# Pooled attention with a gated feed-forward: the order of all instructions read from a table instead of computed by a list scheduler

## The chip, the core and the metric

One core of a Trainium2 chip runs the whole kernel. The metric is device time in microseconds (us). The kernel was timed in three runs; one more execution was profiled, and all rows below come from that one.

## What is computed

Queries are averaged over pairs of neighbouring positions, attention is computed for 4 batches of 8 heads (1152 keys, 576 pooled queries, 64 wide), and the result goes through a feed-forward network with a convolution of three taps and a sigmoid gate:

```python
q_pool = q.reshape(B, H, S // 2, 2, D).mean(axis=3)
scores = (1 / np.sqrt(D)) * np.matmul(q_pool, k.transpose(0, 1, 3, 2))
attn = softmax(scores)                      # max, exp, divide by the sum
x = np.matmul(attn, v) -> (B, 576, 512)     # heads side by side
h = np.maximum(x @ w_in, 0.0)               # 512 -> 1024
conv_out[s] = sum_k conv_w[k] * h[s + k - 1]
out = (h * sigmoid(conv_out)) @ w_out       # 1024 -> 512
```

## The kernel before

The work is cut into 2149 tasks. A task belongs to one engine and issues one instruction or a short run of them (a DMA task belongs to SP, whose queue issues all DMAs). Sixteen pairs of heads are handled one after the other, four to a batch; pairs overlap in time.

For each pair SP loads keys (`load_k`), queries (`load_q`) and values (`load_v`). `sum_q` adds the two neighbouring queries, `keep_q` scales them, `swap` copies them by DMA to the other half of the partitions (tile `qd`). Nine blocks of scores follow. For each block PE writes 128 x 1152 scores into PSUM tile `s` (line 474), DVE takes the row maximum (`top`, line 486), ACT the exponential (`expo`, line 491), and then the slot of `s` is free again. `s` has two slots, so the third block's matmuls wait for the first block's exponential. DVE turns sums into reciprocals (`inverse`, lines 504 and 508).

The probabilities must then be transposed. For most heads ACT or POOL writes a float16 high part (`high`: line 533 on ACT, line 528 on POOL), DVE the low part (`low`, line 536), and SP transposes both by DMA (line 549). For the seven heads in `X32` the block is normalised in float32 (`norm`, line 568, POOL or DVE), PE transposes it (line 581) and ACT copies it out of PSUM tile `a` (line 586). `values` multiplies with V (lines 611 and 617). Values are split into high and low parts too (`abs_v`, `spread_v`, `top_v`, `hi_v`, `lo_v`).

When four pairs are done, `feed` multiplies with `w_in` (line 652) and does relu, `tap0` (ACT or POOL), two more taps (line 675), tanh and the gate; `second` multiplies with `w_out` (line 718 and 724), copies out (`keep`, line 732) and stores. Before that, 17 pieces of weights are converted from 64-bit to 32-bit floats by `weights`: a load, then ACT `size`, DVE `clamp` and three `bits` (lines 784, 793, 798, 802), ACT `rest`, DVE `join` (line 815), POOL `join` (line 817).

Every engine executes its tasks strictly in one fixed order. `Plan.order` makes that order when the program is built: every task has a key (a constant of `AT` plus the number of its pair), a duration written by hand, and its dependences; a list scheduler picks, again and again, the ready task of the lowest key on the engine that can begin first, and gives each buffer the slot that comes free first. Which of the tasks that could run on two engines go where is set by the lists `HIGH` and `MORE`. A buffer taken again waits for all users of the slot's last holder.

Of the kernel before, what the change touches and what calls it, by code (L numbers as in the profile page):

```python
# [16 lines left out]

# [12 lines left out]
class Ring:  # L30


    def __init__(self, name, n, pool, shape, dtype, lead=False):
        self.name, self.n, self.pool, self.shape, self.dtype = name, n, pool, shape, dtype
        self.slots = [None] * n
        self.queue = []
        self.lead = lead


class Buf:  # L40


    def __init__(self, ring, order=None):
        self.ring, self.users, self.slot, self.t = ring, [], None, None
        self.order = order
# [12 lines left out]
class Task:  # L58
    def __init__(self, key, engine, ns, fn, after=(), uses=(), takes=(), port=False, dma=0.0, mode=0):
        self.key, self.engine, self.ns, self.fn = key, engine, ns, fn  # L60
        self.after, self.uses, self.takes = list(after), list(uses), list(takes)
        self.port, self.dma, self.mode = port, dma, mode
        self.start = self.end = None
        for b in self.uses + self.takes:
            b.users.append(self)


class Plan:


    HOP = 0.09
    LOOK = 0.25
    SWITCH = 0.1
    DRAIN = 0.05
# [9 lines left out]
    def order(self):  # L84
        free = {}
        mode = 0
        dma = 0.0
        held = {"POOL": 0.0, "DVE": 0.0}
        other = {"POOL": "DVE", "DVE": "POOL"}
        left = sorted(self.tasks, key=lambda t: t.key)  # L90
        for t in left:
            for b in t.takes:
                for u in b.users:
                    if u is not t and t not in u.after:
                        u.after.append(t)
        for n, t in enumerate(left):
            t.rank = n
            t.wait = len(t.after)
            t.ready = 0.0
            t.next = []  # L100
        for t in left:
            for a in t.after:
                a.next.append(t)
        for t in left:
            for b in t.takes:
                b.ring.queue.append(b)
        ready = [t for t in left if not t.wait]
        done = []

        def slot_time(t):  # L110
            worst, picks, used = 0.0, [], {}
            for b in t.takes:
                r = b.ring
                k = used.get(r, 0)
                if r.lead and r.queue[k] is not b:
                    return None
                used[r] = k + 1
                best = None
                for i, old in enumerate(r.slots):
                    if (r, i) in picks:  # L120
                        continue
                    if old is None:
                        at = 0.0
                    elif any(u.end is None for u in old.users):
                        continue
                    else:
                        at = max(u.end for u in old.users) + self.HOP
                    if best is None or at < best[0]:
                        best = (at, i)
                if best is None:  # L130
                    return None
                picks.append((r, best[1]))
                worst = max(worst, best[0])
            return worst, picks

        while ready:
            could = []
            for t in ready:
                s = slot_time(t)
                if s is None:  # L140
                    continue
                at = max(t.ready, s[0], free.get(t.engine, 0.0))
                if t.port:
                    at = max(at, held[other[t.engine]])
                could.append((at, t, s[1]))
            if not could:
                raise RuntimeError("no task can begin: " + ", ".join(str(t.key) for t in ready[:9]))
            first = {}
            for at, t, p in could:
                e = first.get(t.engine)  # L150
                if e is None or at < e:
                    first[t.engine] = at
            pick = min(
                (c for c in could if c[0] <= first[c[1].engine] + self.LOOK),
                key=lambda c: (
                    first[c[1].engine],
                    c[1].key - (AT["stay"] if c[1].engine == "PE" and c[1].mode == mode else 0.0),
                    c[1].rank,
                ),
            )  # L160
            at, t, picks = pick
            t.start = at
            busy = at + t.ns
            if t.engine == "PE":
                busy += self.SWITCH * (t.mode != mode)
                mode = t.mode
            if t.port:
                held[t.engine] = busy
            free[t.engine] = busy
            t.end = busy  # L170
            if t.dma:
                dma = max(dma, at + 1.4) + t.dma
                t.end = dma + 1.1
            for b, (r, i) in zip(t.takes, picks):
                b.slot = i
                r.slots[i] = b
                r.queue.remove(b)
            ready.remove(t)
            done.append(t)
            for n in t.next:  # L180
                n.wait -= 1
                hop = self.HOP if n.engine != t.engine or t.dma else 0.0 if n.engine == "PE" else 0.08
                if t.engine == "PE" and n.engine != "PE":
                    hop += self.DRAIN
                n.ready = max(n.ready, t.end + hop)
                if not n.wait:
                    ready.append(n)
        if len(done) != len(left):
            raise RuntimeError("tasks left")
        done.sort(key=lambda t: t.start)  # L190
        return done

AT = {
    "first_v": -552.65, "load": -571.72, "load_v": -328.63, "turn_k": -136.13, "turn_q": -82.52,
    "abs_v": -120.27, "hi_v": -89.34, "lo_v": -340.13, "sum_q": 171.08, "turn_p": -295.04, "mm": -898.8,
    "top": 127.29, "exp": -1.46, "inv": 15.15, "high": -11.73, "low": -9.95, "pv": -231.88, "f1": 62.48,
    "f1_step": 0.05, "f2": 240.2, "f2_step": 157.77, "g1": 86.75, "g1_step": 0, "g2": 97.99, "g2_step": 0.4,
    "end": 82.52, "wi": 3.33, "wi_step": 3.68, "wo": 29.25, "wo_step": 10.18, "stay": 246.22,
}

HIGH = [1, 0, 3, 3, 1, 4, 0, 3, 9, 3, 0, 0, 0, 0, 3, 1]

MORE = {
    "norm": [8, 5, 3, 9, 9, 8, 8, 3, 8, 8, 8, 5, 2, 7, 9, 0],
    "tap0": [6, 2, 4, 1, 0, 7, 1, 7],
    "hi_v": [1, 0, 0, 1, 0, 1, 1, 0, 0, 0, 0, 1, 1, 1, 1, 0],
    "sum_q": [1, 1, 1, 1, 0, 0, 0, 0, 1, 1, 1, 1, 1, 0, 0, 1],  # L210
}
X32 = {(0, 0), (1, 0), (2, 0), (3, 1), (4, 1), (5, 1), (8, 0)}
# [3 lines left out]
def tile_pooled_attention_conv_gate_ffn(  # L216
# [10 lines left out]
    nc = tc.nc  # L227
# [30 lines left out]
    r_s = Ring("s", 2, ps, [P, 3 * 512], F32, lead=True)  # L258
    r_a = Ring("a", 2, ps, [P, 512], F32)
    r_vin = Ring("vin", 1, sb, [P, 2, NC, D], F32, lead=True)  # L260
    r_qin = Ring("qin", 1, sb, [P, 2, K0], F32, lead=True)
    r_kt = Ring("kt", 3, sb, [P, S], F32, lead=True)
    r_qt = Ring("qt", 2, sb, [P, K0], F32, lead=True)
    r_qd = Ring("qd", 2, sb, [P, K1], F32, lead=True)
    r_v = Ring("v", 2, sb, [P, 2, NC, P], F16, lead=True)
    r_p = Ring("p", 3, sb, [P, S], F32, lead=True)
    r_hl = Ring("hl", 4, sb, [P, 2, S], F16, lead=True)
    r_pt = Ring("pt", 4, sb, [P, 2 * NC, 320], F16, lead=True)
    r_sm = Ring("sm", 4, sb, [P, 8], F32, lead=True)
    r_vs = Ring("vs", 3, sb, [P, 8], F32, lead=True)  # L270
    r_x = Ring("x", 7, sb, [P, 578], F32, lead=True)
    r_h = Ring("h", 5, sb, [P, 324], F32)
    r_g = Ring("g", 4, sb, [P, 4, 322], F32, lead=True)
# [20 lines left out]
    for pr in range(NPAIR):  # L294
        o = Pair()
        o.b, o.h0, o.k0 = pr // NP, 2 * (pr % NP), 9 * pr
        o.pr, o.vin, o.qin = pr, Buf(r_vin), Buf(r_qin)
        o.kt, o.qt, o.qd = Buf(r_kt), Buf(r_qt), Buf(r_qd)

        o.x32 = [(pr, e) in X32 for e in range(2)]  # L300
        o.v, o.vs = Buf(r_v), Buf(r_vs)
        o.x = Buf(r_x)
        pairs.append(o)

    def loads(o):
        k0 = o.k0
# [14 lines left out]
        lk = [add(k0 + AT["load"], "SP", 0.3, load_k, takes=[o.kt], dma=2.1)]  # L321
# [431 lines left out]
    def weights(src, j, c, key, ready):  # L753
# [67 lines left out]
        if key > AT["wi"]:  # L821
            gated.append(t)
# [101 lines left out]
```

## Time and profile before

| what | us |
|---|---|
| median of three runs | 677.12 (674.49 to 678.02) |
| the profiled execution, its own time | 677.61 |
| its span, first to last instruction | 675.6 |
| mean granted TensorE clock, share of 2.4 GHz | 0.975 |

Two microseconds lie outside the span. An engine's busy time is the time in which at least one of its instructions runs; instructions overlap a little, so sums of durations are some per cent above it. A wait is put down to the instruction that came last.

### The profile page before, as it was taken

The page shows a single profiled execution, that of the slowest core. Times are in us where ns is not written, and L with a number is a line of the kernel's source. Part 1 is how long each engine was busy: PE and PEld are TensorE (multiplying, and loading weights), DVE is VectorE, ACT ScalarE, POOL GpSimd, SP SyncE. Part 2 cuts the span into 40 slices and gives each one's busy share as a digit, 9 for nine tenths or more (in the row PEclk, how much of TensorE's full clock was granted, in tenths as well). Part 3 has the DMA queues.
Part 4 walks back from the last instruction along what each step waited for, and adds up shares of the span by engine and source line. Part 5 has one row for each costly group of instructions (what it writes and reads, how often), then busy time and mean ns, then how long its engine had stood idle before and what let it go on. Part 6 is the DMA issues. An engine that isn't in the chain of part 4 may idle for free.

```text
span 675.6 us, 10454 instructions
## 1 busy us (share of the span) xinstructions
PE 628.2 (93%) x3805; PEld 385.2 (57%) x3805; DVE 538.0 (80%) x797; ACT 477.7 (71%) x789; POOL 161.9 (24%) x183
## 2 busy tenths in 40 slices
PE   4778788899989999999999899999999999999997
PEld 2455555465656656456666566556666655568643
DVE  3888887889899899977889899888788999745610
ACT  3898856688878888676777787876868777745401
POOL 2543423234452412115433010010100412000200
PEclk9899976699999999999999999999999999999999
DMA  7897956569696699799989989899898999991001
GB/s 271 214 199 137 249 142 169 122 158 211 130 216 166 134 209 204 124 209 201 188 159 228 185 171 211 145 229 200 176 211 164 188 178 168 179 178 38 0 16 54
DMA packets 279123, 113.72 MB, mean 168 GB/s; under 512 B 265377, under 2 KB 265889, under 8 KB 279073
## 3 DMA queue, kind: packets, MB, share of 16 engines
q1 hardware_dynamic: 279072, 113.07, 80.1%
q8 instruction: 30, 0.49, 0.3%
q14 instruction: 21, 0.16, 0.1%
HBM read 37.77 MB, written 4.72 MB: 63 GB/s over the span
## 4 chain that ended last, share of the span: by engine, by line
PE 67%; DVE 12%; ACT 11%; issue 5%; DMA 3%; POOL 1%; SPq 0%; ACTq 0%; DVEq 0%; POOLq 0%
PE s L474 19%; PE a L718 16%; PE a L652 13%; PE a L611 10%; ACT p L491 5%; PE a L617 5%; DVE sm L486 4%; DVE hl L536 4%; PE a L581 3%; ACT pt L586 2%; PE a L724 2%; ACT hl L533 2%; DVE g L675 1%; DMA pt<-hl 1%; DMA qd<-qt 1%
## 5 line engine op out<-in xcount | busy, mean ns | idle before, releaser
L474 PE MATMUL s<-kt,qt 64*128 64x512 f32 (+3 forms) x704 | 192.1, 486 | 31.9 <-ACT p L491 24.0
L486 DVE TENSOR_REDUCE sm<-s 128x1 f32<-128x1152 f32 x144 | 193.1, 1350 | 28.8 <-PE s L474 28.0
L491 ACT ACTIVATE p<-s,sm 128x1152 f32<-128x1152 f32 x144 | 175.1, 1217 | 57.6 <-DVE sm L486 34.6
L536 DVE SCALAR_TENSOR_TENSOR hl<-p,sm,hl 128x1152 f16<-128x1152 f32 (+1 forms) x116 | 167.6, 1457 | 14.2 <-ACT hl L533 9.7
L474 PEld LDWEIGHTS s<-kt,qt 64*128 64x128 f32 (+1 forms) x704 | 92.0, 178 | 148.0 <-issue 87.1
L474 PE MATMUL s<-kt,qd 64*128 64x512 f32 x256 | 147.4, 662 | 0.2 <-DMA qd<-qt 0.2
L652 PE MATMUL a<-x,wi 128*128 128x257 f32 (+1 forms) x512 | 135.0, 414 | 1.8 <-ACT x L624 1.1
L533 ACT ACTIVATE hl<-p,sm 128x1152 f16<-128x1152 f32 (+1 forms) x96 | 118.5, 1247 | 9.3 <-issue 3.2
L611 PE MATMUL a<-pt,v 128*64 128x256 f16 (+1 forms) x1350 | 121.6, 291 | 0.3
L718 PE MATMUL a<-wo,g 128*128 128x512 f32 x256 | 116.8, 600 | 0.0
L652 PEld LDWEIGHTS a<-x,wi 128*128 128x128 f32 x512 | 93.8, 189 | 31.4 <-issue 1.9
L611 PEld LDWEIGHTS <-v 128*64 128x64 f16 x1350 | 89.3, 111 | 14.9 <-issue 5.6
L675 DVE SCALAR_TENSOR_TENSOR g<-h,cw,g 128x255 f32<-128x255 f32 (+1 forms) x128 | 63.6, 516 | 23.3 <-POOL g L668 11.9
L718 PEld LDWEIGHTS a<-wo,g 128*128 128x128 f32 x256 | 46.7, 190 | 50.1 <-issue 46.6
L617 PE MATMUL a<-pt,v 128*64 128x256 f32 (+1 forms) x252 | 67.4, 424 | 0.0
L586 ACT ACTIVATE pt<-a 128x384 f32<-128x384 f32 (+2 forms) x98 | 43.8, 477 | 24.6 <-PE a L581 24.3
L568 POOL TENSOR_SCALAR p<-p,sm 128x1152 f32<-128x1152 f32 (+1 forms) x31 | 41.5, 1340 | 68.7 <-DVE sm L508 48.4
L581 PE MATMUL a<-ident,p 128*128 128x128 f32 (+1 forms) x315 | 49.2, 288 | 7.9 <-ACT pt L586 4.7
L668 POOL TENSOR_SCALAR g<-h,cw 128x321 f32<-128x321 f32 (+1 forms) x28 | 20.7, 742 | 137.5 <-ACT h L658 121.0
L658 ACT ACTIVATE h<-a 128x257 f32<-128x257 f32 (+1 forms) x64 | 25.9, 408 | 30.4 <-PE a L652 28.8
L581 PEld LDWEIGHTS a<-ident,p 128*128 128x128 f32 (+1 forms) x315 | 34.1, 149 | 19.6 <-ACT pt L586 9.7
L528 POOL TENSOR_SCALAR hl<-p,sm 128x1152 f16<-128x1152 f32 (+1 forms) x20 | 26.4, 1321 | 67.3 <-DVE sm L508 39.1
(56 smaller groups left out, 488.7 us busy)
## 6 DMA issues: line engine op xcount, KB each, us to landing
qin<-in_q_dram SPq DMA_DIRECT2D x16, 640.0 KB, 5.9
kt<-in_k_dram SPq DMA_DIRECT2D x16, 576.0 KB, 4.8
vin<-in_v_dram SPq DMA_DIRECT2D x9, 576.0 KB, 4.9
g<-in_moe_w_in_dram SPq DMA_DIRECT2D x8, 512.0 KB, 5.2
qd<-qt SPq DMA_DIRECT2D x32, 128.0 KB, 6.4
g<-in_moe_w_out_dram SPq DMA_DIRECT2D x8, 512.0 KB, 4.2
out_dram<-o SPq DMA_DIRECT2D x16, 256.0 KB, 2.6
vin<-in_v_dram SPq DMA_DIRECT2D x7, 288.0 KB, 3.3
```

The source lines that it names most:

```text
L474: nc.tensor.matmul(out=w, lhsT=f, rhs=kk, start=True, stop=True)
L486: nc.vector.tensor_reduce(out=sm[:, e:e + 1], in_=runs(st[e]), axis=AX.XY, op=ALU.max, negate=True)
L491: nc.scalar.activation(out=p.tile().rearrange("p (a n) -> p a n", a=2), in_=runs(st[e]), func=AF.Exp, bias=sm[:, e:e + 1], scale=1.0, accu ...
L533: nc.scalar.activation(out=hl[rows, 0], in_=ps_[e][rows], func=AF.Copy, scale=sm[rows, 6 + e:7 + e])
L536: nc.vector.scalar_tensor_tensor(out=hl[rows, 1], in0=ps_[e][rows], scalar=sm[rows, 6 + e:7 + e], in1=hl[rows, 0], op0=ALU.mult, op1=ALU.s ...
L581: nc.tensor.transpose(w[:, (i - a1) * nq:(i - a1 + 1) * nq], ps_[e][rows, i * P:(i + 1) * P], ident[rows, rows])
L586: nc.scalar.activation(out=pt.tile().rearrange("p a n -> p (a n)").bitcast(F32) .rearrange("p (a n) -> p a n", a=NC)[:, a1:a2, c:c + nq], ...
L611: nc.tensor.matmul(out=to, lhsT=o.v[:, e, c, vc:vc + D], rhs=o.pt[y, e][:, hl * NC + c, 0:n], start=(c == 0 and j == 0), stop=(c == NC - 1 ...
L617: nc.tensor.matmul(out=to, lhsT=o.v[:, e, c].bitcast(F32), rhs=p32.rearrange("p (a n) -> p a n", a=NC)[:, c, 0:n], start=(c == 0), stop=(c ...
L652: nc.tensor.matmul(out=w[:, 0:n], lhsT=wi[:, j, f * P:(f + 1) * P], rhs=x.x[:, 255 * u:255 * u + n], start=(j == 0), stop=(j == KC - 1),)
L675: nc.vector.scalar_tensor_tensor(out=c, in0=h[:, t:t + tok], scalar=cw[:, f, t:t + 1], in1=c, op0=ALU.mult, op1=ALU.add)
L718: nc.tensor.matmul(out=w.tile(), lhsT=g[f // 4][:, f % 4, c:c + P], rhs=wo[:, f, :], start=(f == 0), stop=(f == FC - 1),)
```

## The change

Keys, costs of hops and the list scheduler go. The order of all tasks stands in a string `ORDER` (two letters per task, by the number in which tasks are created), the slot of each buffer in a string of 1040 digits `SLOTS`, and 94 tasks that run on their second engine in `SWAPPED`. Tasks that have two possible engines carry the second in `alt`; the POOL `join` of the weights gets one too (DVE). The set `X32` still has seven heads, two of them others. What is computed, how much of it, and the number and sizes of the buffers stay.

```diff
-    def order(self):
-        free = {}
...
-        done.sort(key=lambda t: t.start)
-        return done
-
-AT = {
-    "first_v": -552.65, "load": -571.72, "load_v": -328.63, "turn_k": -136.13, "turn_q": -82.52,
...
-X32 = {(0, 0), (1, 0), (2, 0), (3, 1), (4, 1), (5, 1), (8, 0)}
+        for i in unpack(SWAPPED):
+            t = self.tasks[i]
+            t.engine = t.alt[0]
+        bufs = [b for t in self.tasks for b in t.takes]
+        for b, slot in zip(bufs, SLOTS):
+            b.slot = int(slot)
+        return [self.tasks[i] for i in unpack(ORDER)]
+
+
+LETTERS = string.ascii_letters + string.digits
+
+
+def unpack(words):
+    words = "".join(words.split())
+    return [62 * LETTERS.index(a) + LETTERS.index(b) for a, b in zip(words[0::2], words[1::2])]
+
+
+ORDER = """
+abw4aaaeafw5agw6w7w8w9xaxbaqacynadbPbNxdbMatarasauaHxcavaKawaIaEaxaiaFaCaJajaLbQaGyoaYaDakaMypyqalbRa1aNaZaOxe
...
+SLOTS = (
+    "00000010100011001001012110001020112111230321101030000011110011101011102001011120021102131022100031000201031111"
...
+SWAPPED = """
+aeaobmb0dCeAeHfugcgqgGgZhjhxh5iiisiEiSjtjTkdkqkTk0lblLl8mbmimDm3ndnqntn5n8omoUo8pnqPrXsksxsUsXtftZuxuHuRu4vhvk
...
+X32 = {(0, 0), (1, 0), (2, 0), (3, 0), (4, 1), (5, 1), (9, 1)}
...
-        t = add(k0 + AT["sum_q"], "POOL" if on_pool else "DVE", 1.52 if on_pool else 0.8, sum_q, after=lq, uses=[o.qin],
-                port=True)
+        t = add("POOL", 1.52, sum_q, after=lq, uses=[o.qin], port=True, alt=("DVE", 0.8, True))
...
-        t = add(key + 1.0, "POOL", 0.05 + m / 415.0, lambda: join(1), after=[t], uses=both, port=True)
+        t = add("POOL", 0.05 + m / 415.0, lambda eng: join(1, eng), after=[t], uses=both, port=True,
+                alt=("DVE", dve(m) - 0.05, True))
...
         for t in order:
-            t.fn()
+            if t.alt:
+                t.fn({"PE": nc.tensor, "DVE": nc.vector, "ACT": nc.scalar, "POOL": nc.gpsimd}[t.engine])
+            else:
+                t.fn()
```

## Rows read from the trace of the kernel before

**Rows 1.** Part 1 of the page: busy us (share of the span) and count of instructions.

```profile
PE 628.2 (93%) x3805; PEld 385.2 (57%) x3805; DVE 538.0 (80%) x797; ACT 477.7 (71%) x789; POOL 161.9 (24%) x183
```

**Rows 2.** Stretches: us, busy by engine, PEclk, DMA share, GB/s; the reduction ending the first.

```profile
8.00:296.70 288.70, 257.55 (x1584) 159.43 (x1582) 251.19 (x374) 226.98 (x385) 99.01 (x94) 0.94 0.80 180
296.70:675.60 378.90, 369.80 (x2224) 225.24 (x2222) 286.70 (x423) 248.05 (x402) 60.43 (x75) 1.00 0.82 158
...
297.01 1.34 DVE L486 TENSOR_REDUCE sm<-s 128x1 f32<-128x1152 f32 x1
```

**Rows 3.** Waits of PE from 8 to 297: us, times, longest.

```profile
PE s L474 <- ACT p L491: 23.1, 23, 2.0
...
PE a L581 <- ACT pt L586: 3.8, 12, 0.6
PE a L581 <- POOL p L568: 2.1, 3, 1.1
```

**Rows 4.** Waits of DVE from 8 to 297, the three largest within it.

```profile
DVE sm L486 <- PE s L474: 14.5, 14, 2.2
...
DVE hl L536 <- ACT hl L533: 5.5, 7, 1.1
DVE sm L504 <- ACT p L491: 5.0, 9, 1.4
```

**Rows 5.** Waits of PE from 297 to the end, first and last of five.

```profile
PE a L724 <- ACT o L732: 1.2, 1, 1.2
...
PE a L652 <- ACT pt L586: 0.3, 1, 0.3
```

**Rows 6.** Groups by line and shape: busy us, mean ns of one, idle before.

```profile
L536 DVE SCALAR_TENSOR_TENSOR hl<-p,sm,hl 128x1152 f16<-128x1152 f32 x109 | 157.7, 1459 | 12.8 <-ACT hl L533 8.6 <-POOL hl L528 3.2
...
L533 ACT ACTIVATE hl<-p,sm 128x1152 f16<-128x1152 f32 x90 | 111.0, 1246 | 8.8 <-issue 3.2 <-DVE sm L508 2.6 <-ACT o L732 1.0
...
L815 DVE TENSOR_TENSOR g<-g 128x512 f32<-128x512 f32 x16 | 11.2, 702 | 2.9 <-ACT g L808 2.8
...
L817 POOL TENSOR_TENSOR wi<-g,wi 128x512 f32<-128x512 f32 x8 | 12.5, 1565 | 28.2 <-DVE g L815 28.0
...
L504 DVE SCALAR_TENSOR_TENSOR sm<-sm,small 128x2 f32<-128x2 f32 x64 | 10.6, 165 | 12.7 <-ACT p L491 11.2
...
L508 DVE RECIPROCAL sm<-sm 128x2 f32<-128x2 f32 x64 | 10.6, 166 | 2.2
...
L344 DVE TENSOR_TENSOR qin<-qin 128x640 f32<-128x640 f32 x6 | 4.9, 814 | 0.0
...
L378 DVE TENSOR_REDUCE vs<-a 128x1 f32<-128x128 f32 x16 | 4.6, 287 | 1.7 <-PE a L373 1.6
...
L568 DVE TENSOR_SCALAR p<-p,sm 128x1152 f32<-128x1152 f32 x3 | 2.4, 816 | 0.1
```

**Rows 7.** DVE in order of time: four conversions of one weight piece, first and last.

```profile
27.50 0.42 DVE L784 TENSOR_SCALAR g<-g 128x512 f32<-128x512 f32 x1
...
29.14 0.43 DVE L802 TENSOR_SCALAR g<-wi 128x512 int32<-128x512 int32 x1
```

**Rows 8.** Two stretches with DVE busiest: columns as in rows 2.

```profile
152.00:169.00 17.00, 15.47 (x86) 10.06 (x86) 16.51 (x27) 13.93 (x25) 8.50 (x9) 1.00 0.91 212
203.00:270.00 67.00, 64.54 (x416) 41.51 (x415) 62.79 (x93) 57.06 (x97) 18.51 (x20) 1.00 0.82 178
```

**Rows 9.** ACT at the start, in order of time.

```profile
4.79 1.28 ACT L347 ACT_TABLE_LOAD   x1 [4.79 <-DMA qin<-in_q_dram]
...
6.36 0.74 ACT L347 ACTIVATE qt<-qin 128x640 f32<-128x640 f32 x1 [0.28 <-POOL qin L344]
```

**Rows 10.** DMA issues on the page: KB each, median us to landing.

```profile
out_dram<-o SPq DMA_DIRECT2D x16, 256.0 KB, 2.6
```

**Rows 11.** PE near the end, in order of time.

```profile
640.30 27.63 PE L718 MATMUL a<-wo,g 128*128 128x512 f32 x64
```

**Rows 12.** Line 536: least, median and longest ns.

```profile
L536 DVE SCALAR_TENSOR_TENSOR hl<-p,sm,hl x116: 1403/1410/2685, 20.1 to 600.3; 128x1152 f16<-128x1152 f32 x109, 64x1152 f16<-64x1152 f32 x7
```

More of the change, by code (lines that the diff above doesn't have):

```diff
@@ L30, with __init__ @@
 class Ring:
-    def __init__(self, name, n, pool, shape, dtype, lead=False):
+    def __init__(self, name, n, pool, shape, dtype):
         self.name, self.n, self.pool, self.shape, self.dtype = name, n, pool, shape, dtype
-        self.slots = [None] * n
-        self.queue = []
-        self.lead = lead
 class Buf:
-    def __init__(self, ring, order=None):
+    def __init__(self, ring):
         self.ring, self.users, self.slot, self.t = ring, [], None, None
-        self.order = order
     def __getitem__(self, key):
@@ L58, with __init__ @@
 class Task:
-    def __init__(self, key, engine, ns, fn, after=(), uses=(), takes=(), port=False, dma=0.0, mode=0):
-        self.key, self.engine, self.ns, self.fn = key, engine, ns, fn
+    def __init__(self, engine, ns, fn, after=(), uses=(), takes=(), port=False, dma=0.0, mode=0, alt=None):
+        self.engine, self.ns, self.fn = engine, ns, fn
         self.after, self.uses, self.takes = list(after), list(uses), list(takes)
-        self.port, self.dma, self.mode = port, dma, mode
-        self.start = self.end = None
+        self.port, self.dma, self.mode, self.alt = port, dma, mode, alt
         for b in self.uses + self.takes:
@@ L84, in order @@
     def order(self):
-        free = {}
[L86 to L187, printed above, removed]
@@ L351, in swap @@
             nc.sync.dma_start(out=o.qd[h], in_=o.qt[g, 0:K1])
[L353 to L356 removed]
+        t = add("POOL", 1.52, sum_q, after=lq, uses=[o.qin], port=True, alt=("DVE", 0.8, True))
+        tq = add("ACT", act(K0, 0.18), keep_q, after=[t], uses=[o.qin], takes=[o.qt])
+        sw = add("SP", 1.0, lambda: [swap(e) for e in range(2)], after=[tq],
                  uses=[o.qt], takes=[o.qd], dma=0.8)
@@ L427, in zero_x @@
             nc.gpsimd.memset(o.x[:, 0:578:577], 0.0)
-        o.zx = add(k0 + 3, "POOL", 0.1, zero_x, takes=[o.x])
+        o.zx = add("POOL", 0.1, zero_x, takes=[o.x])
         if not two:
@@ L508, in inverse @@
             nc.vector.reciprocal(out=sm[:, 6:6 + n], in_=sm[:, 4:4 + n])
-        iv = add(i0 + n + AT["inv"], "DVE", 0.265, inverse, after=ex, uses=[sm], port=True)
+        iv = add("DVE", 0.265, inverse, after=ex, uses=[sm], port=True)
         y = int(d > 1)
@@ L539, in low @@
                     )
-                t = add(i0 + n + e + AT["high"], "POOL" if on_pool else "ACT", 1.22 if on_pool else act(S, 0.1), high,
-                        after=[iv], uses=[ps_[e], sm], takes=[hl], port=on_pool)
-                t = add(i0 + n + e + AT["low"], "DVE", dve(S) - 0.025, low, after=[t], uses=[ps_[e], sm, hl], port=True)
+                t = add("ACT", act(S, 0.1), high, after=[iv], uses=[ps_[e], sm], takes=[hl],
+                        alt=("POOL", 1.22, True))
+                t = add("DVE", dve(S) - 0.025, low, after=[t], uses=[ps_[e], sm, hl], port=True)
             for h in by_dma:
@@ L571, in norm @@
                     )
-                td = add(i0 + n + e + AT["high"], "POOL" if on_pool else "DVE", 1.28 if on_pool else 0.08 + S / 1900.0, norm, after=[iv],
-                         uses=[sm, ps_[e]] + ([] if new else [pt]), takes=[pt] if new else [], port=True)
+                td = add("POOL", 1.28, norm, after=[iv], uses=[sm, ps_[e]] + ([] if new else [pt]),
+                         takes=[pt] if new else [], port=True, alt=("DVE", 0.08 + S / 1900.0, True))
                 groups = ((0, 5), (5, 9)) if m else ((0, 3), (3, 6), (6, 9))
@@ L630, in values, with feed @@
         for i in range(1):
-            t = add(key + 0.1 * i, "PE", (n * 27.0 / 2400 * (4 / 3 if any(o.x32) else 1) + 0.08), lambda i=i: part(i), mode=2,
+            t = add("PE", (n * 27.0 / 2400 * (4 / 3 if any(o.x32) else 1) + 0.08), lambda i=i: part(i), mode=2,
                     after=o.turned[y] + o.vls + ([t] if t else []),
                     uses=[o.v, o.pt[y, 0], o.pt[y, 1]] + ([w] if i else []), takes=[] if i else [w])
-        o.xs.append(add(key + 0.3, "ACT", act(n, 0.1), keep, after=[t, o.zx], uses=[w, o.x] + ([] if all(o.x32) else [o.vs])))
+        o.xs.append(add("ACT", act(n, 0.1), keep, after=[t, o.zx], uses=[w, o.x] + ([] if all(o.x32) else [o.vs])))
     TOK = (255, 321)
-    def feed(b, u, k1, f_step):
+    def feed(b, u):
         tok = TOK[u]
@@ L689, in feed, with second @@
             first = f % 4 == 0
-            t = add(key, "PE", 16 * n / 2400.0 + 0.03, mm, after=need + wi_ready[f // 4], uses=[x.x for x in xs], takes=[w])
-            t = add(key + 0.5, "ACT", act(n), relu, after=[t], uses=[w], takes=[h])
-            t = add(key + 0.6, "POOL" if on_pool else "ACT", 0.28 + tok / 1400.0 if on_pool else act(tok, 0.07), tap0, port=on_pool, after=[t] + cw_ready, uses=[h] + ([] if first else [g]),
+            t = add("PE", 16 * n / 2400.0 + 0.03, mm, after=need + wi_ready[f // 4], uses=[x.x for x in xs], takes=[w])
+            t = add("ACT", act(n), relu, after=[t], uses=[w], takes=[h])
+            t = add("ACT", act(tok, 0.14), tap0, alt=("POOL", 0.28 + tok / 1400.0, True), after=[t] + cw_ready, uses=[h] + ([] if first else [g]),
                     takes=[g] if first else [])
-            t = add(key + 1.0, "DVE", dve(tok), lambda tap=tap: tap(1), after=[t], uses=[h, g], port=True)
-            t = add(key + 1.1, "DVE", dve(tok), lambda tap=tap: tap(2), after=[t], uses=[h, g], port=True)
-            t = add(key + 1.5, "ACT", act(tok, 0.04), tanh, after=[t], uses=[g])
-            done.append(add(key + 2.0, "DVE", dve(tok) - 0.06, gate, after=[t], uses=[h, g], port=True))
+            t = add("DVE", dve(tok), lambda tap=tap: tap(1), after=[t], uses=[h, g], port=True)
+            t = add("DVE", dve(tok), lambda tap=tap: tap(2), after=[t], uses=[h, g], port=True)
+            t = add("ACT", act(tok, 0.04), tanh, after=[t], uses=[g])
+            done.append(add("DVE", dve(tok) - 0.06, gate, after=[t], uses=[h, g], port=True))
         return gs, done
-    def second(b, gs, done, key, step, t):
+    def second(b, gs, done, t):
         u = int(t > 1)
@@ L710, in edge @@
                 )
-            need += [add(key - 0.5, "POOL", 0.25, lambda i=i: edge(i), port=True, after=done[0] + done[1],
+            need += [add("POOL", 0.25, lambda i=i: edge(i), port=True, after=done[0] + done[1],
                          uses=[gs[0][i], gs[1][i]]) for i in range(2)]
@@ L742, in second @@
         for i in range(4):
-            last = [add(key + i * step / 4, "PE", 1.73 if t < 4 else 0.88, lambda i=i: mm2(i), mode=0 if t < 4 else 2,
+            last = [add("PE", 1.73 if t < 4 else 0.88, lambda i=i: mm2(i), mode=0 if t < 4 else 2,
                         after=need + last + wo_ready, uses=g + ([w] if i else []), takes=[] if i else [w])]
-        e = add(key + step, "ACT", act(n), keep, after=last, uses=[w], takes=[o])
-        add(key + step + 0.1, "SP", 0.4 if t < 4 else 0.8, store, after=[e], uses=[o], dma=0.9)
+        e = add("ACT", act(n), keep, after=last, uses=[w], takes=[o])
+        add("SP", 0.4 if t < 4 else 0.8, store, after=[e], uses=[o], dma=0.9)
     wi_ready = [[], []]
@@ L816, in join @@
             else:
-                nc.gpsimd.tensor_tensor(out=a, in0=mm, in1=a, op=ALU.add)
+                eng.tensor_tensor(out=a, in0=mm, in1=a, op=ALU.add)
         both = [raw, tmp]
-        t = add(key, "SP", 0.4, load, takes=[raw], dma=1.7)
-        if key > AT["wi"]:
+        t = add("SP", 0.4, load, takes=[raw], dma=1.7)
+        if src is not w_in or j or c:
             gated.append(t)
-        t = add(key + 0.3, "ACT", act(m, 0.08), size, after=[t], uses=[raw], takes=[tmp])
-        t = add(key + 0.4, "DVE", 0.08 + m / 1900.0, clamp, after=[t], uses=[tmp], port=True)
+        t = add("ACT", act(m, 0.08), size, after=[t], uses=[raw], takes=[tmp])
+        t = add("DVE", 0.08 + m / 1900.0, clamp, after=[t], uses=[tmp], port=True)
         for n in range(3):
-            t = add(key + 0.5 + 0.05 * n, "DVE", (dve(m) - 0.05 if n == 1 else 0.08 + m / 1900.0), lambda n=n: bits(n), after=[t], uses=both, port=True)
-        t = add(key + 0.8, "ACT", act(m, 0.08), rest, after=[t], uses=both)
-        t = add(key + 0.9, "DVE", dve(m) - 0.05, lambda: join(0), after=[t], uses=both, port=True)
-        t = add(key + 1.0, "POOL", 0.05 + m / 415.0, lambda: join(1), after=[t], uses=both, port=True)
+            t = add("DVE", (dve(m) - 0.05 if n == 1 else 0.08 + m / 1900.0), lambda n=n: bits(n), after=[t], uses=both, port=True)
+        t = add("ACT", act(m, 0.08), rest, after=[t], uses=both)
+        t = add("DVE", dve(m) - 0.05, lambda: join(0), after=[t], uses=both, port=True)
+        t = add("POOL", 0.05 + m / 415.0, lambda eng: join(1, eng), after=[t], uses=both, port=True,
+                alt=("DVE", dve(m) - 0.05, True))
         ready.append(t)
@@ L839, in tile_pooled_attention_conv_gate_ffn @@
             values(o, y)
-    n = 0
     for c in range(2):
         for j in range(KC):
-            weights(w_in, j, c, AT["wi"] + AT["wi_step"] * n, wi_ready[c])
-            n += 1
-    weights(conv_w, 0, 0, AT["wi"] + AT["wi_step"] * n, cw_ready)
-    n += 1
+            weights(w_in, j, c, wi_ready[c])
+    weights(conv_w, 0, 0, cw_ready)
     for j in range(FC):
-        weights(w_out, j, 0, AT["wo"] + AT["wo_step"] * j, wo_ready)
+        weights(w_out, j, 0, wo_ready)
     for b in range(B):
-        last = pairs[b * NP + NP - 1].k0
-        early = AT["end"] * (b == B - 1)
-        done = [
-            feed(b, 0, last + AT["f1"], AT["f1_step"]),
-            feed(b, 1, last + AT["g1"] + early, AT["g1_step"]),
-        ]
-        gs, done = zip(*done)
-        second(b, gs, done, last + AT["f2"], AT["f2_step"], 0)
-        for i, t in enumerate((1, 2, 3, 4)):
-            second(b, gs, done, last + AT["g2"] + early + i * AT["g2_step"], AT["g2_step"], t)
+        gs, done = zip(feed(b, 0), feed(b, 1))
+        for t in range(5):
+            second(b, gs, done, t)
     for t in gated:
```

180 lines of the change are left out of this document (100 added, 80 removed).

## The prediction

> **What bounds the kernel now.** I read the page first. PE is busy 93% of the span, DVE 80%, ACT 71% [rows 1]. Shares over the whole span hide the stages, so I next asked for two stretches, cut at the first reduction of pair 8 (297 us) and starting at 8 us, when the first scores are under way [rows 2]. Up to the cut PE is busy 257.6 of 288.7 us (89.2%) and DVE 251.2 (87.0%), with ACT at 227: three engines feed each other and none is full. After the cut PE is busy 369.8 of 378.9 us, 97.6%, at full granted clock, and most of the 9.1 us that are left is the tail of the last copy and store. So time can be won almost only ahead of the cut.
>
> Who is waited for there comes from the waits. PE's idle time ahead of the cut is mostly one kind: 23.1 us in 23 waits of scores for an exponential, against 3.8 and 2.1 us for the next two [rows 3]. Scores wait for it because tile s has two slots, and a slot is free when the exponential of its last block has been read out. The exponential waits for the reduction on DVE, and that for the scores: DVE's own largest wait is 14.5 us for scores, then 5.5 us for the high part on ACT and 5.0 us for the sums of an exponential [rows 4]. It is a loop through PE, DVE and ACT, and what stretches it is other work that stands between its steps in the fixed order of DVE and ACT. After the cut PE has five kinds of waits, 1.2 us down to 0.3, together 4.4 us [rows 5].
>
> **The change, part by part.** The list scheduler runs when the program is built, so taking it away costs no device time. What changes is the order on each engine, the slots, and where the movable tasks run. I decoded the table by numbering the tasks in order of creation, and set it against the order in the trace of before.
>
> *PE's order.* Up to the first scores of pair 8 both orders hold the same PE tasks, to the last one: 72 blocks of scores, 84 groups of transposes, 14 value products, 16 of the 64 first products of the feed-forward, 8 quarters of the second. Only neighbours change places. So pair 8's scores are one milestone with the same PE work ahead of it in both, and the table has to reach it sooner.
>
> *DVE's work ahead of that milestone grows.* Seven of the seventeen weight additions move from POOL to DVE, all of them among the sixteen of full size. The trace has no such addition on DVE; the nearest row is the other join of the same size there, 0.702 us, and the far bound is what it takes on POOL, 1.565 us. I take 0.70: same engine, same operation with two inputs in SBUF, same shape. Seven make +4.9 us (11.0 at the far bound). Three more normalisations come to DVE (7 instead of 4): 3 x 0.816 = +2.4. One more sum of queries: +0.8. One reduction for the scale of values stands earlier: +0.3. Two low parts and one pair of reciprocal steps stand later: -2 x 1.459 - (0.165 + 0.166) = -3.2 [rows 6]. Sum: 4.9 + 2.4 + 0.8 + 0.3 - 3.2 = +5.2 us, 256.4 instead of 251.2. ACT gives five high parts away there, 5 x 1.246 = -6.2 us [rows 6], and takes three smaller tasks; POOL's total of movable tasks over the whole kernel stays 114 (high 20 to 38, the weight additions 17 to 10, norm 31 to 27, tap0 28 to 24, query sums 10 to 7, values 8 and 8).
>
> So by load alone the table makes the early part worse: at DVE's present share of 87.0% the milestone would come after 256.4 / 0.870 = 294.7 us instead of 288.7. It comes equally late at a share of 256.4 / 288.7 = 88.8%, and sooner only above.
>
> *What raises the share.* In the old order the five DVE instructions of a weight piece mostly stand in a block. One piece shows it: from 27.50 to 29.57 us DVE converts, four instructions in a row [rows 7], and a reduction, its exponential and the next scores stand behind them. Counted in the orders, the 85 such DVE instructions before form 37 runs, ten of them four or longer; in the table 92 form 57 runs, four of them that long, and the first piece for w_out is spread between the first reductions. A long run broken up takes up to two microseconds out of the loop and puts filler where DVE waits. How full DVE can be in this kernel is seen in two stretches: 16.51 of 17 us (97.1%) from 152 to 169, and 62.79 of 67 (93.7%) from 203 to 270 [rows 8]. I take 92%, a little under the longer of the two: 256.4 / 0.92 = 278.7, a gain of 10.0 us. The other way to size it is PE's 23.1 us [rows 3]: if half goes, 11.5. I take the middle, 10.8.
>
> *After the cut* the two orders hold the same PE work; half of the 4.4 us of waits is 2.2. ACT's load falls there too, but PE is the bound, so that is worth nothing more.
>
> *The start.* The first sum of queries moves from POOL to DVE, 0.814 us. POOL is no longer ahead of ACT then, but the load of ACT's table is: it ends at 4.79 + 1.28 = 6.07 and the scaling now begins at 6.36 [rows 6, 9]. The gain is 0.3 us at most; loading the first weights ahead of the keys can take it away again, so nothing to 0.3.
>
> *The end.* The last batch's first three outputs all take one slot of the output tile, so each copy waits for the store before it. That store lands 2.6 us after its issue [rows 10]; between those copies the table has six and then three quarters of output products, at 27.63 / 16 = 1.73 us each [rows 11], so 10.4 and 5.2 us of cover for a store and the copy ahead of it. It costs nothing; without the cover it would be at least 2.6 us for each of the two.
>
> *Contention of POOL and DVE.* Line 536 takes 1.410 us in the median and 2.685 at worst, its full-width form 1.459 in the mean: 109 x 0.049 = 5.3 us lost over the whole kernel, although 114 POOL tasks run beside it [rows 6, 12]. The Trainium skill ("SBUF — State Buffer", Who interferes with whom) says that a DVE instruction with two SBUF inputs and a reading GpSimd instruction shut each other out for their full length, the later one waiting. By that rule the 18 high parts that go to POOL could each hold up a low part; the rows show such a hold as the exception. This is rival D.
>
> **Sum.** 677.6 (the profiled execution) - 10.8 - 2.2 - 0.3 = 664.3, so 664 us; against the median of 677.1 it is 1.9% less.
>
> **Rivals.**
>
> A, *the early loop closes almost fully*. DVE holds the 97.1% of its best stretch up to pair 8: 256.4 / 0.971 = 264.1, a gain of 24.6, with 2.5 for the rest 650 us. For it: the mean granted clock is 0.94 ahead of the cut and 1.00 after [rows 2], so PE is slow there for a part of the time, with idle gaps in front; fewer gaps can bring clock back as well. 0.06 x 289 = 17 us of clock are missing. Against it: PE would have to be busy 257.6 of 264, unless that clock does come back.
>
> B, *the added DVE work decides*. The order fits hand-written durations no better than the old one did, the share stays at 87.0%, and the milestone comes 6.0 us late: 677.6 + 6.0 = 683.6, nothing given back later since PE is full there. It decides at any share under 88.8%, only 1.8 points above today's. For it: an engine that runs in fixed order loses all that a late producer costs, and loads of weights and weight work are drawn forward (the first w_out piece is the second one converted). Against it: the broken runs.
>
> C, *the order is nearly the old one, and what is won early is lost as small waits in the full part*. For it: PE's sequences differ only among neighbours, DVE has more to do, and behind the cut any new wait costs its full length, since PE is 97.6% busy there. The 13 us won are lost again by a dozen waits of about a microsecond, and the time is 677. Against it: PE's five kinds of waits there are short today with an order made by the same rules [rows 5].
>
> D, *the shared port*. After pair 8, 13 more high parts run on POOL and 4 fewer other movable tasks, net 9. If each of the 13 holds a low part by 2.685 - 1.410 = 1.275 us [rows 12], DVE loses 16.6 us there. DVE is idle 378.9 - 286.7 = 92 us in that part [rows 2], so it costs nothing until the held low parts stand in the loop; with all of it on the path the sum is 664.3 + 16.6 = 681. It decides from the point at which those low parts, and not PE, set the next step.
>
> **How the numbers follow.** The forecast has 0.52, A 0.18, B 0.16, C 0.12, D 0.02. No change means within 0.5% (3.4 us), about what a measurement of this kernel can tell; the three runs spread by that much. Forecast and A are faster: 0.70. B and D are slower, 0.18, and C is the same, 0.12. The range goes from a little under A (647) to B (684); the forecast's own runs from 656 (share 95%) to 671 (share 90%). The far bound of the weight additions, +6.1 us of DVE work, lies inside it.
>
> **What the profile after would show.** Right: PE's wait of scores for an exponential ahead of pair 8 at about half of 23 us; DVE's share up to that milestone above 90%, with seven weight additions on DVE at about 0.7 us; pair 8's first reduction near 286 us; PE's share after it unchanged at 97 to 98%. Wrong: the milestone at 297 or later (B), or earlier by 10 us while PE's waits after it grow by as much (C); line 536 with a mean well above 1.46 us (D). A new wait that would upset the sum is one for a DMA, of which PE hardly has any today: the transposes share one queue with weights that are now loaded earlier.

## The result

The changed kernel takes 653.4 us in the median of four runs (651.5 to 655.3) against 677.4 for the kernel before, a ratio of 0.9653 with a 95% interval of 0.961 to 0.970. The profiled execution has a span of 649.5 us, 26.1 less than before, and takes 651.47 us. Line numbers are those of the changed file: scores 404, reductions 416, exponentials 421, low parts 463, transposes 506, weight additions 738.

The page's busy times [rows 1 for before]:

```profile
PE 612.6 (94%) x3805; PEld 380.1 (59%) x3805; DVE 535.5 (82%) x811; ACT 453.0 (70%) x775; POOL 158.7 (24%) x183
```

PE's own busy time fell by 15.6 us although it does the same matmuls, and ACT's by 24.7; DVE's is nearly what it was (2.5 us less).

Where the 26.1 us came from is read at pair 8's first scores, ahead of which PE has the same tasks in both kernels. PE in order of time, before:

```profile
294.69 0.69 PE L474 MATMUL s<-kt,qt 64*128 64x512 f32 x1
```

after:

```profile
272.97 0.69 PE L404 MATMUL s<-kt,qd 64*128 64x512 f32 x1
```

That point comes 21.7 us sooner. The stretches up to it and behind it (columns as in rows 2), before:

```profile
0.00:294.69 294.69, 256.39 (x1572) 158.66 (x1572) 249.24 (x374) 227.81 (x384) 101.47 (x108) 0.94 0.79 180
...
294.69:675.60 380.91, 371.81 (x2235) 226.50 (x2233) 288.71 (x424) 249.86 (x406) 60.43 (x75) 1.00 0.82 159
```

after:

```profile
0.00:272.97 272.97, 243.43 (x1574) 152.89 (x1574) 247.19 (x383) 219.69 (x380) 82.86 (x96) 0.98 0.84 192
8.00:272.97 264.97, 243.38 (x1574) 152.82 (x1574) 245.45 (x379) 217.04 (x377) 82.16 (x90) 0.98 0.84 191
272.97:649.50 376.53, 369.14 (x2235) 227.16 (x2233) 288.31 (x428) 233.30 (x396) 75.84 (x88) 1.00 0.81 163
```

Ahead of the point PE's records count 1572 matmuls in both kernels (two more are under way at the second cut). Its busy time falls from 256.4 to 243.4 us (13.0), its idle time from 294.7 - 256.4 = 38.3 to 29.5 (8.8), and the granted clock rises from 0.94 to 0.98. Behind it the same work takes 376.5 instead of 380.9 us, another 4.4; PE is busy 98.0% of that.

Waits of PE up to that point, after [rows 3]:

```profile
PE s L404 <- DMA kt<-in_k_dram: 8.0, 1, 8.0
PE s L404 <- ACT p L421: 6.9, 12, 1.4
PE a L506 <- ACT pt L511: 6.4, 13, 1.3
PE a L506 <- POOL p L493: 5.6, 5, 2.1
```

Scores wait 6.9 us for an exponential where it was 23.1. The transposes wait more: 6.4 and 5.6 us against 3.8 and 2.1. The first scores wait for the keys until 7.96 us.

The waits behind it, first and last of four, together 3.0 us [rows 5]:

```profile
PE s L404 <- ACT p L421: 1.8, 4, 0.5
...
PE a L306 <- ACT pt L511: 0.3, 1, 0.3
```

DVE's waits from 8 to 275 us, the start of pair 8's first reduction [rows 4]:

```profile
DVE sm L433 <- ACT p L421: 5.9, 8, 1.4
DVE sm L416 <- PE s L404: 4.1, 9, 0.7
...
DVE hl L463 <- ACT hl L460: 0.8, 1, 0.8
```

The 14.5 us of waiting for scores became 4.1, and 5.5 for ACT's high parts became 0.8; only the wait for the sums of an exponential is as long as it was.

Groups by line and shape, after [rows 6]:

```profile
L463 DVE SCALAR_TENSOR_TENSOR hl<-p,sm,hl 128x1152 f16<-128x1152 f32 x109 | 157.9, 1456 | 18.6 <-ACT hl L460 10.6 <-POOL hl L455 6.1 <-POOL x L358 1.4
...
L455 POOL TENSOR_SCALAR hl<-p,sm 128x1152 f16<-128x1152 f32 x36 | 48.6, 1351 | 140.1 <-DVE sm L437 93.9 <-issue 17.1 <-ACT pt L511 7.9
...
L738 DVE TENSOR_TENSOR wo<-g,wo 128x512 f32<-128x512 f32 x4 | 2.7, 684 | 0.0
```

### The profile page after: what moved, and what is told of

Its sections match the earlier page's. It is cut to its first block, busy times and chain, and to the rows that moved or that the text cites. A ratio compares the mean times of both kernels' runs of the same rounds, so it can differ in the third digit from the quotient of the medians.

```text
span 649.5 us, 10435 instructions
## 1 busy us (share of the span) xinstructions
PE 612.6 (94%) x3805; PEld 380.1 (59%) x3805; DVE 535.5 (82%) x811; ACT 453.0 (70%) x775; POOL 158.7 (24%) x183
## 5 line engine op out<-in xcount | busy, mean ns | idle before, releaser
L404 PE MATMUL s<-kt,qt 64*128 64x512 f32 (+3 forms) x704 | 183.2, 471 | 17.2 <-ACT p L421 8.7
L404 PE MATMUL s<-kt,qd 64*128 64x512 f32 x256 | 144.0, 647 | 0.0
L535 PE MATMUL a<-pt,v 128*64 128x256 f16 (+1 forms) x1350 | 118.1, 288 | 0.1
L460 ACT ACTIVATE hl<-p,sm 128x1152 f16<-128x1152 f32 (+1 forms) x78 | 97.0, 1252 | 13.0 <-issue 3.9
L455 POOL TENSOR_SCALAR hl<-p,sm 128x1152 f16<-128x1152 f32 (+1 forms) x38 | 51.0, 1344 | 140.3 <-DVE sm L437 93.9
L596 DVE SCALAR_TENSOR_TENSOR g<-h,cw,g 128x321 f32<-128x321 f32 (+1 forms) x128 | 65.1, 526 | 12.4 <-POOL g L589 8.5
L541 PE MATMUL a<-pt,v 128*64 128x256 f32 (+1 forms) x252 | 64.1, 409 | 0.5 <-ACT pt L511 0.5
L493 POOL TENSOR_SCALAR p<-p,sm 128x1152 f32<-128x1152 f32 (+1 forms) x27 | 37.6, 1394 | 87.6 <-DVE sm L437 68.4
L589 POOL TENSOR_SCALAR g<-h,cw 128x255 f32<-128x255 f32 (+1 forms) x24 | 17.4, 727 | 103.2 <-ACT h L581 92.8
L541 PEld LDWEIGHTS a<-pt,v 128*64 128x64 f32 x252 | 33.4, 137 | 11.1 <-ACT pt L511 1.0
```

Source lines behind the costliest of these rows:

```text
L404: nc.tensor.matmul(out=w, lhsT=f, rhs=kk, start=True, stop=True)
L455: eng.tensor_scalar(out=hl[rows, 0], in0=ps_[e][rows], scalar1=sm[rows, 6 + e:7 + e], scalar2=1.0, op0=ALU.mult, op1=ALU.mult,)
L460: nc.scalar.activation(out=hl[rows, 0], in_=ps_[e][rows], func=AF.Copy, scale=sm[rows, 6 + e:7 + e])
L535: nc.tensor.matmul(out=to, lhsT=o.v[:, e, c, vc:vc + D], rhs=o.pt[y, e][:, hl * NC + c, 0:n], start=(c == 0 and j == 0), stop=(c == NC - 1 ...
L541: nc.tensor.matmul(out=to, lhsT=o.v[:, e, c].bitcast(F32), rhs=p32.rearrange("p (a n) -> p a n", a=NC)[:, c, 0:n], start=(c == 0), stop=(c ...
L596: nc.vector.scalar_tensor_tensor(out=c, in0=h[:, t:t + tok], scalar=cw[:, f, t:t + 1], in1=c, op0=ALU.mult, op1=ALU.add)
```

## The experiments

The order, the slots and the engines of the movable tasks are data, so each experiment is another table, made from the two orders; where a task could not stand at its new place it was put at the next place that its dependences and slots allow. The slots and the two other heads of `X32` go with the order in these runs; neither was changed alone. All were timed beside the kernel before, whose medians were 676.1 to 677.4 us.

| kernel | median us | ratio to before, 95% | pair 8's first scores on PE at |
|---|---|---|---|
| changed kernel | 653.4 | 0.961 to 0.970 | 273.0 |
| new order, old engines | 670.7 | 0.988 to 0.994 | 281.5 |
| old order, new engines | 694.8 | 1.021 to 1.031 | 306.6 |
| new front, old back (second splice) | 663.2 | 0.976 to 0.983 | 272.2 |
| old front, new back (second splice) | 676.6 | 0.997 to 1.002 | 292.4 |
| weight conversions drawn together | 668.1 | 0.984 to 0.991 | 288.3 |
| old order, conversions spread | 697.7 | 1.027 to 1.035 | 314.5 |
| old order with filler matmuls | 676.8 | 0.998 to 1.003 | 292.0 |
| weight additions back on POOL | 650.4 | 0.958 to 0.965 | 275.4 |
| high parts back | 657.3 | 0.968 to 0.974 | 279.0 |
| small moves back | 664.8 | 0.976 to 0.986 | 277.9 |

**Order or engines?**

```diff
-aeaobmb0dCeAeHfugcgqgGgZhjhxh5iiisiEiSjtjTkdkqkTk0lblLl8mbmimDm3ndnqntn5n8omoUo8pnqPrXsksxsUsXtftZuxuHuRu4vhvk
+b0dCd2d9ejeRfugjgGgQgZiiiBiEjTlblllvlLl8mDmQm3ndngnqntnAnWn5n8oUpxtfuxuRu7vuvZv9zzzNzUz1AfAmAtAVBTB7ClCzCNE7Fl
```

(the first line of the list of tasks on their second engine, new order.)

> The new order and slots, but every task that can run on two engines goes to the engine it had before (94 tasks differ; pairs 8 and 9, whose exact head changed places, keep the new choice). Theory 'order': which task stands behind which makes the gain, so this keeps most of it: 653 to 660 us, with the wait of scores for an exponential ahead of pair 8 still below 12 us (before 23.1, after 6.9). Theory 'engines': the 20 us of work taken off ACT and the short weight additions on DVE make it: 665 us or more, and that wait back above 15 us.

> The old order and slots written as a table, with the new choice of engines for the 94 tasks. Theory 'order': little or nothing won, 672 to 682 us, since DVE has 5 us more ahead of pair 8 and stands in the old order. Theory 'engines': 662 us or less.

Neither stands alone. With the old engines the new order wins 6 of 24 us; the new engines in the old order lose 18. The new order with old engines, stretches and waits of PE ahead of pair 8's scores:

```profile
0.00:281.60 281.60, 247.42 (x1574) 154.54 (x1574) 246.94 (x372) 222.90 (x381) 96.24 (x105) 0.98 0.81 186
281.60:668.30 386.70, 372.63 (x2234) 227.66 (x2233) 290.85 (x427) 248.14 (x408) 70.91 (x78) 0.99 0.80 159
```

```profile
PE s L404 <- ACT p L421: 10.8, 21, 1.2
PE a L506 <- POOL p L493: 7.9, 8, 2.0
```

It is 8.6 us late at that point and 10.2 us longer behind it (386.7 against 376.5). Its time would fit a pure "engines" theory (665 us or more), but the sign that this theory was to show, the score wait above 15 us, isn't there (10.8), and the new engines alone, 662 us or less by it, take 694.8; POOL's slower normalisations are waited for longer (7.9 against 5.6). Both theories fall in their pure form.

Three groups of the 94 moves were undone singly.

```diff
-vuvxvEvZwmwpwMwPxcxlxVyNyWzezwzzz1AfAtAAAOCeCGCUC8ErEyEMETFeFlFNGxGEHdHkHFHTH7
+vuvxvEvZwmwpwMwPzzz1AfAtAAAOCeCGCUC8ErEyEMETFeFlFNGxGEHdHkHFHTH7
```

(the seven additions; the other two are made in the same way.)

> The changed kernel with the seven weight additions back on POOL (1.57 us each there, 0.685 on DVE). By the prediction's sum DVE has 4.8 us less ahead of pair 8. If that load decides: 649 to 653 us. If POOL's slower additions stand ahead of normalisations that PE's transposes wait for: 655 to 659.

> The changed kernel with the 35 high parts that changed engine back where they were (net 18 from POOL to ACT). All 94 moves undone cost 17 us. Theory 'ACT's relief': most of that is here, 660 us or more. Rival 'shared between POOL and DVE': moving them off POOL is harmless or helps, 650 to 656.

> The changed kernel with query sums, high parts of values and first taps back on the engines they had (43 tasks). If every move counts alike: about half of the 17 us, 659 to 663. If the large tasks count: 653 to 656.

The additions on POOL give 650.4, 3.0 us less than the changed kernel; the intervals of the two ratios overlap, so this is no measured gain, but nothing shows that moving them to DVE bought anything. The high parts are worth 3.9 us: less than was expected of ACT's relief (660 us or more), a little outside what the rival gave (650 to 656), and with intervals that just overlap. The 43 small moves are worth 11.4 us, more than was expected of either theory. In the profiled execution, which is 15.1 us longer than the changed kernel's, 5.0 are lost ahead of pair 8's scores and 10.2 behind them. There PE waits 11.0 us instead of 3.0, most of all for exponentials:

```profile
PE s L404 <- ACT p L421: 6.0, 8, 1.9
```

Which of the 43 moves does it was not found. The nine moves of normalisations were not undone alone, and the three groups sum to 12.3 of the 17.3 us of all moves.

**Front or back?** The first pair of splices renamed the heads of pair 3 and thereby changed some ten places of DVE's order in each:

> New order and engines for all tasks that stand ahead of the first scores of pair 8, old order and engines for the rest (old set of exact heads). Theory 'front': on PE's own order those scores begin 21.7 us earlier in the changed kernel, and only 4.4 us are won behind them, so this gives 677.4 - 21 = 656 us, 653 to 661. Rival 'back': the front's lead is lost again with the old order behind it: 665 us or more.

> The mirror image: old order and engines ahead of the first scores of pair 8, new ones behind. Theory 'front': 677.4 - 4 = 673 us, 669 to 677. Rival 'back': 665 us or less.

They took 673.4 and 686.9 us, and the first had lost ten us of its lead by the start of pair 4, so they tell little about the front. The second pair has no such change:

```diff
-X32 = {(0, 0), (1, 0), (2, 0), (3, 0), (4, 1), (5, 1), (9, 1)}
+X32 = {(0, 0), (1, 0), (2, 0), (3, 0), (4, 1), (5, 1), (8, 0)}
```

(for the new front with the old back, besides the order; the other has heads 1 of pairs 3 and 9.)

> The new order and engines for all that stands ahead of pair 8's first scores, the old ones behind, with a set of exact heads that fits both halves (the changed kernel's for pairs 0 to 7, the old one's for 8 to 15), so that no engine's order has to be changed at the seam. In the earlier splice heads of pair 3 were renamed and the lead was lost there, by the start of pair 4. Theory 'front': pair 8's scores start at about 273 us on PE and the total is 655 to 661. Rival 'the parts are coupled': the scores start there, and the lead of 21 us is lost again behind the seam, 665 or more.

> The mirror image with the same care: old front, new back. Theory 'front': 669 to 677 us, pair 8's scores at about 295. Rival 'coupled': 680 or more, as in the earlier splice (686.9), since the back finds its producers at other times than it was ordered for.

The new front does bring pair 8's scores at 272.2 us, and the total keeps 13 of the 22.5 us. The stretches of that kernel:

```profile
0.00:272.10 272.10, 244.50 (x1572) 153.00 (x1572) 247.15 (x383) 219.72 (x380) 82.59 (x96) 0.99 0.83 191
272.10:300.00 27.90, 22.95 (x120) 12.75 (x116) 17.48 (x27) 14.12 (x24) 8.39 (x13) 0.88 0.95 194
```

In the 28 us behind the seam PE is idle for 5.0 us and the granted clock is at 0.88. This fits an old back that finds its producers at other times than in the kernel that it was ordered for; no run shows that reason by itself. The old front with the new back gains nothing in time. "Front" is right about the place of the gain, "coupled" about the price of a seam.

**Do broken runs of weight conversions do it?**

```diff
 DVE, changed kernel and the first piece of w_out
-wo0.clamp wo0.b0 least_v inv max pow_v max low wo0.b1 wi01.clamp lo_v wo0.b2
+least_v inv max pow_v max low lo_v wo0.clamp wo0.b0 wo0.b1 wo0.b2
 DVE, kernel before and the second piece of w_in
-wi01.clamp wi01.b0 wi01.b1 wi01.b2 inv max join low max
+wi01.clamp inv wi01.b0 max wi01.b1 low wi01.b2 max join
```

(DVE's order in short names of its tasks.)

> The changed kernel, in which only DVE's conversions of a weight piece are drawn together again: clamp and the first two bits stand right ahead of the third, so that 15 runs of four or more stand in DVE's order instead of 4. Theory 'broken runs': this takes a good part of the early gain away, 658 to 664 us, and the wait of scores for an exponential ahead of pair 8 rises from 6.9 to 12 us or more. Rival: the runs did not matter, the time stays within 653 plus or minus 3 us.

> The kernel before (order, slots, engines), in which only DVE's runs of weight conversions are broken: another DVE task is put between every two of them, so that 78 runs stand in place of 37 and none is longer than three. What waits for a conversion on ACT and POOL moves with it where it must. Theory 'broken runs are enough': drawing them together in the new order cost 14.7 us, so this wins 6 to 12 us, 664 to 670. Rival 'only within an order made for it': within 3.4 us of 676, since ACT's conversions still stand where they stood.

Drawn together they cost 14.7 us, more than the 5 to 11 expected. But spread in the old order they cost 20.5 us, where a gain was expected. The first kernel's waits of DVE and ACT up to its pair 8's scores (288.3 us):

```profile
DVE sm L433 <- ACT p L421: 14.2, 11, 2.1
```

```profile
ACT p L421 <- DVE sm L416: 22.7, 17, 3.0
...
ACT g L729 <- DVE wo L719: 5.7, 3, 2.7
ACT g L729 <- DVE wi L719: 4.4, 3, 2.1
```

The same for ACT in the changed kernel, up to 273 us:

```profile
ACT p L421 <- DVE sm L416: 19.4, 16, 3.0
...
ACT g L729 <- DVE wi L719: 1.7, 1, 1.7
```

The scores' wait rises only to 9.9 us, under the 12 expected. What grows is DVE's wait for exponentials (14.2 us instead of 5.9) and ACT's wait in line 729, its own conversion step, for DVE's conversions: 10.1 us instead of 1.7. The conversions that were drawn together stand later in DVE's order, and ACT's step stayed where it was. On PE the transposes wait 21.1 us instead of 12.8.

The second kernel, ACT in order of time:

```profile
15.85 0.66 ACT L729 ACTIVATE g<-g 128x512 f32<-128x512 uint32 x1 [7.67 <-DVE wi L719]
16.41 1.21 ACT L421 ACTIVATE p<-s,sm 128x1152 f32<-128x1152 f32 x1
```

ACT's own conversion step (line 729) stands ahead of the first exponential in ACT's order, as in the kernel before, where it waits 1.74 us. Here it waits 7.67 us for DVE, whose conversions now come one by one between reductions, and up to 300 us such waits sum to 11.5 us, against 2.3 before:

```profile
ACT g L729 <- DVE wi L719: 11.5, 5, 7.7
```

So the loop that the spreading was to free is held up on the other engine; scores then wait for exponentials for longer than before (28.9 us against 23.1):

```profile
PE s L404 <- ACT p L421: 28.9, 22, 4.0
```

Both edits put conversions at later places and left ACT's step where it stood. They do not tell the length of a run from the hold-up of ACT, and a spreading that takes ACT's step along was not tested.

**Does the clock do it?**

```diff
         for t in order:
...
                 t.fn()
+            for _ in range(FILL.get(plan.tasks.index(t), 0)):
+                nc.tensor.matmul(out=t.takes[0][:, 384:512], lhsT=ident, rhs=ident, start=True, stop=True)
```

> The kernel before (its order, slots and engines as a table) with 54 additional matmuls of 128 columns that nobody reads, in ten of the places ahead of pair 4 in which PE waited for an exponential, as many as fit into each wait. No wait is shortened by itself. Theory 'clock': PE's granted clock falls after such gaps, so with them filled the granted clock up to 295 us rises from 0.94 to 0.97 or more and the time falls by 3 to 8 us, to 669 to 674. Rival 'the gaps do not set the clock' : clock unchanged, time 677 to 683.

The stretch to pair 8's scores, and the fillers in it:

```profile
0.00:292.10 292.10, 257.54 (x1682) 164.66 (x1682) 248.57 (x374) 227.92 (x384) 102.10 (x108) 0.99 0.80 182
```

```profile
L787 PE MATMUL a<-ident 128*128 128x128 f32 x108 | 13.8, 276 | 0.0
```

The granted clock is 0.99 instead of 0.94, as expected: it falls after PE's gaps. PE is busy 257.5 us, of which the fillers' group has 13.8, so its own work takes about 12.7 us less than before; yet the point comes only 2.7 us sooner, and the time is unchanged where 3 to 8 us less were expected. Behind seven of the ten filled places PE still waits 0.1 to 1.8 us for an exponential, so the fillers do not stand in its way there. A faster PE is worth little while DVE and ACT set the pace.

## Why the prediction was right, and where it was off

It said 664 us, range 647 to 684, faster; measured 653.4. The direction and the bound were right, the size was not. The time lies nearer to rival A (650) than to the forecast, and below the forecast's own runs (656 to 671); the range holds it only because it reaches down to rival A, whose condition, a share of 97.1% on DVE, did not come about. So that the range holds it is in part luck.

- *The bound.* Right: 21.7 of 26.1 us were won ahead of pair 8's scores, and PE is still full behind. Half of 4.4 us of waits was taken as gain there; the waits fell by 1.4 us, PE's busy time by 2.7, and the gain is 4.4 instead of 2.2. The new small waits of rival C did not come. (Of the 9.1 us that PE was idle there before, the tail is 4.1, since PE ends at 671.5 of 675.6 us; that is not most of it.)
- *The term that was off in size: the gain up to the milestone, 10.8 us, measured 22.0.* Pair 8's first reduction was forecast near 286 us; it moved from 297.0 to 275.0, about as much as the scores ahead of it:

```profile
274.97 1.34 DVE L416 TENSOR_REDUCE sm<-s 128x1 f32<-128x1152 f32 x1
```

```profile
8.00:274.97 266.97, 245.38 (x1581) 154.00 (x1582) 247.02 (x382) 218.75 (x381) 84.16 (x91) 0.98 0.84 191
```

The share of DVE was right: it rose from 87.0% to 247.02 / 266.97 = 92.5%, where 92% was taken. The work was wrong: 247.0 us instead of 256.4. With it the forecast's own share gives 247.0 / 0.92 = 268.5 us, a gain of 20.2. The tasks were counted rightly, but their whole durations were added to a busy time, in which overlapping time counts once. Up to pair 8's scores DVE's groups sum to 263.5 us before and 267.0 after, 3.5 more; its busy time is 249.2 and 247.2 us (0:294.69 and 0:272.97 above), so the overlap grew from 14.3 to 19.8. In a run of conversions each instruction needs the one before and begins 0.03 us behind its end. Before:

```profile
27.50 0.42 DVE L784 TENSOR_SCALAR g<-g 128x512 f32<-128x512 f32 x1
27.95 0.43 DVE L793 TENSOR_SCALAR wi<-g 128x512 int32<-128x512 int32 x1
```

In the following lines, where the neighbour is other work, each begins 0.08 to 0.09 us ahead of that end. After:

```profile
25.18 0.68 DVE L719 SCALAR_TENSOR_TENSOR wo<-g,wo 128x512 int32<-128x512 int32 x1
25.78 0.42 DVE L705 TENSOR_SCALAR g<-g 128x512 f32<-128x512 f32 x1
26.11 0.81 DVE L352 SCALAR_TENSOR_TENSOR v<-vin,vs,v 128x576 f16<-128x576 f32 x1
```

The kernel with the conversions drawn together shows the same the other way: the same 383 instructions keep DVE busy for 253.8 us, 6.6 more. Of these 3.4 are lost overlap (its groups sum to 270.2) and 3.2 are longer instructions.

```profile
0.00:288.30 288.30, 247.78 (x1572) 154.48 (x1572) 253.76 (x383) 220.65 (x380) 81.10 (x96) 0.97 0.79 182
```

- *PE's view of it.* Half of 23.1 us was taken; 16.2 went. The transposes, a wait that I did not count, took 6.1 us of that back.
- *Rival A's clock.* 13.0 us of PE's busy time went with the higher clock. The fillers show that filled gaps bring the clock back, and that this is not by itself a gain.
- *The reason given for the share.* Only half of it stands. Drawing the runs together in the new order costs 14.7 us; breaking them in the old one costs 20.5. In both ACT's conversion step is held up, which the prediction did not count.
- *Weight additions.* Priced at 0.70 us, measured 0.685. Undoing them changes the time by 3.0 us at most, within the intervals.
- *The start.* Scaling begins at 5.70 instead of 6.36 us, of which 0.4 is an earlier landing of the queries, but the first scores come 0.8 us later, because the keys are loaded behind weights:

```profile
4.41 1.28 ACT L281 ACT_TABLE_LOAD   x1 [4.41 <-DMA qin<-in_q_dram]
5.70 0.74 ACT L281 ACTIVATE qt<-qin 128x640 f32<-128x640 f32 x1
...
7.96 1.19 PE L404 MATMUL s<-kt,qt 64*128 64x512 f32 x1 [7.96 <-DMA kt<-in_k_dram]
```

- *The end.* No wait of the output matmuls is left; the old 1.2 us for a copy is gone, and the three outputs in one slot cost nothing.
- *Rival B* did not come about with this order. With the old one its mechanism is what the new engines do (694.8): from 8 us to pair 8's scores DVE is busy 258.72 of 298.60 us, a share of 86.6%, 9.5 us more of busy time than before.

```profile
8.00:306.60 298.60, 260.83 (x1571) 161.88 (x1570) 258.72 (x383) 222.21 (x379) 88.43 (x86) 0.93 0.77 172
```

- *Rival D.* The full-width low parts' mean is 1456 ns against 1459, with 18 more high parts on POOL; the seven with 64 rows rose from 1414 to 1579, 1.2 us in all. The rule of the Trainium skill ("SBUF — State Buffer", Who interferes with whom) would let the two hold each other up; the mean shows no more of it than before.

## What to carry to other kernels

When engines run in a fixed order, order and choice of engine are one decision: a table made for one choice lost most of its gain with another, and a good half lost part of it at a seam. A busy time counts overlapping time once, so durations can't simply be added to it: the same instructions keep an engine busy for longer where each needs the one before, and for less where independent ones follow each other. Before crediting a rule such as "spread the conversions", follow the chain to the engine that it passes through: it has its place in that order too.

## What was not expected of the hardware

Four runs of the changed kernel show how far the clock and the time go together without any change of code: spans of 649.5, 650.2, 652.5 and 653.3 us at mean granted clocks of 0.992, 0.990, 0.984 and 0.987. And 54 matmuls whose results nobody reads raised the granted clock over 292 us from 0.94 to 0.99 without a gain in time.
